# Linear attention, MoE and FFN on one core: the FFN's second weights converted during the MoE, and each expert's first product issued one branch earlier

## The chip, the cores and the metric

One core of a Trainium2 chip runs the whole program in one launch. The metric is the device time of one execution in microseconds (us). TensorE (PE) multiplies matrices, VectorE (DVE), ScalarE (ACT) and GpSimd (POOL) do elementwise work, SyncE (SP) issues DMA transfers, and ACT and POOL issue some too. Each engine works through its own instructions in order and waits on semaphores for the others.

## The reference

Three stages follow each other. Attention is linear: softmax of q over the head's elements, softmax of k over the sequence, `kv = k^T v`, and `q kv` per head. Its output, 4608 tokens of 512 elements, is the input of a mixture of experts: tokens with `x @ w_skip > 0` go to the expert with the highest gate logit,

```python
for e in range(8):
    h = np.maximum(xc[mask] @ w1[e], 0.0)          # 512 -> 1024
    y[mask] = gate_w[mask, None] * (h @ w2[e])     # 1024 -> 512
out[do_compute] = xc + y
```

and then comes a feed-forward network (FFN) over all tokens:

```python
h = x @ w_in                                        # 512 -> 2048
g = np.maximum(h, 0.0) + np.log1p(np.exp(-np.abs(h)))
return (g @ w_out).astype(np.float32)               # 2048 -> 512
```

The weights `w_in` and `w_out` come as 64-bit floats, passed as 64-bit integers. They have to be made float32 on the chip before they can be multiplied.

## The kernel before, in words

Every product is made of three: each operand is split into a high part h (rounded) and a low part l (the rest), and h·h, h·l and l·h are summed in PSUM. So each tile of tokens or weights costs an ACT copy (the high part) and a subtraction on DVE or POOL (the low part): `hilo` L494 to L498 for tokens, `split` L465 to L471 for an expert's weights, in eight pieces of 1024 columns.

Attention ends with a routing step that counts the tokens of each expert and scatters the rows into `xs` in DRAM, sorted by expert. The counts are known only at run time, so each expert is a tree of branches (`tiles`): tiles of 128 tokens are taken in pairs, and a branch asks whether there is another pair, another single tile, or none. On the given data the experts e0 to e7 have 4, 1, 2, 3, 1, 6, 5 and 8 tiles, which makes 2, 1, 1, 2, 1, 3, 3 and 4 pairs (a lone tile is counted as a pair here). For a pair, `mm1` (four steps of 24 matmuls, L522; for a lone tile `mm1one`, two halves of 12, L535) makes the hidden values in four PSUM banks `mph`; ACT's Relu and a DVE operation make their parts `mhT`, where a lone tile goes through the buffer `mh` first (Relu L536). Then `mm2` (L548 to L550) makes `mpy`, DVE adds it to the token rows (L553), and POOL scatters them back to `xs` (L555). While expert e computes, the weights of e+1 are split, a few pieces at a time, at places (`tick`) inside `mm1` and `mm2`; the order of all instructions is the order of the code. The weights of e+2 are loaded into the same staging buffers as they come free.

A 64-bit weight is converted by `Convert` (L416 to L433): two ACT operations (Abs and a copy of the low words, L423 and L424), four on DVE (L428 to L431) and two on POOL (L432, L433). The `w_in` words are converted in e7 by `cv`, 16 steps of 512 columns. The `w_out` words are converted in the FFN, again 16 steps of 512, one in each of the first 16 of its steps.

The FFN takes nine blocks of 512 tokens, each with 16 steps of 128 hidden columns, 144 steps in all. A step is `mm1` (12 matmuls L690), the softplus (three ACT operations L692 to L694, four DVE operations L697 to L701), the parts `gh` (ACT, L708) and `gl` (L712), and `mm2` of two steps earlier (12 matmuls each of L720 to L722). In the first 16 steps `mid` and `end` put in the conversion: `hi` L745 and `lo` L747 make the parts of a converted piece of `w_out`, `begin` and `end` (L748 to L751) convert another, and `rawload` L743 fetches 512 KB of words.

Of the kernel before, what the change touches and what calls it, by code (L numbers as in the profile page):

```python
# [76 lines left out]
def attention(tc, ctx, q, k, v, wg, xs, ident, consts):  # L77
    nc=tc.nc
# [309 lines left out]
    def finish(p):  # L388
# [22 lines left out]
        return nv,fence(list(writes)),others  # L411
# [5 lines left out]
class Convert:  # L417
# [7 lines left out]
    def rest(s):  # L425
        t,H,L=s.t,s.H,s.L; ti=t.bitcast(I32); Hf=H.bitcast(F32); Lf=L.bitcast(F32)
        v=s.nc.vector; p=s.nc.gpsimd
        v.tensor_scalar(t,t,LEAST,None,op0=ALU.max)  # L428
        v.tensor_scalar(ti,ti,3,0x3ffffff8,op0=ALU.logical_shift_left,op1=ALU.bitwise_and)  # L429
        v.scalar_tensor_tensor(out=ti,in0=H,scalar=-0x40000000,in1=ti,op0=ALU.bitwise_and,op1=ALU.bitwise_or)  # L430
        v.tensor_scalar(H,ti,-0x800000,None,op0=ALU.bitwise_and)  # L431
        p.tensor_tensor(out=Hf,in0=Lf,in1=Hf,op=ALU.mult)  # L432
        p.tensor_tensor(out=t,in0=t,in1=Hf,op=ALU.add)  # L433


KLV=5
LAG=3
ALL=[getattr(mybir.EngineType,x) for x in ("PE","Activation","DVE","Pool","SP")]
class Moe:
    def __init__(s, tc, ctx, xs, wsets, w64, ident, slotpool, spare, KLV=KLV):  # L440
        s.tc=tc; s.nc=tc.nc; s.xs=xs; s.users={}; s.w=wsets; s.ident=ident; s.w64=w64; s.K=KLV
# [38 lines left out]
    def cv(s,k=1):  # L480

        for _ in range(k):
# [44 lines left out]
    def mm1one(s,e,tick=lambda:None,between=lambda:None):  # L527

        nc=s.nc; wh,wl=s.slot[e]; xh,xl=s.xT[:,0,0],s.xT[:,1,0]
        for half in range(2):  # L530
            p=s.ph()
            ops=[(kc,x,w) for kc in range(4) for x,w in ((xh,wh),(xh,wl),(xl,wh))]
            if half==0: ops.sort(key=lambda o:o[1] is xl)
            for n,(kc,x,w) in enumerate(ops):
                nc.tensor.matmul(p,x[:,kc*128:kc*128+128],w[:,kc*1024+half*512:kc*1024+half*512+512],start=(n==0),stop=(n==11))  # L535
            nc.scalar.activation(s.h[:,half*512:half*512+512],p,AF.Relu)  # L536
            tick()
        for q in range(2):
            p=s.ph()
# [18 lines left out]
    def tiles(s,e,i,t):  # L558
# [3 lines left out]
        def second(last=None):  # L562
            for j in range(t): s.mm2(e,x[j],j,tick)
            if i==0: s.pieces(16)
            if last: last()
        def next():
            if i==0: s.late(e)
            s.first(e+1)
        if t==1:
            s.mm1one(e,tick,next); s.hint(e+1)  # L570
# [4 lines left out]
        def more(k):  # L575
            y=s.pair(e,i+1)
            for j in range(k): s.loadx(e,i+1,j)
            if i==0: s.late(e)
# [276 lines left out]
```

## Time and profile before

| | us |
|---|---|
| median of 3 runs | 1438.57 |
| lowest, highest | 1432.34, 1439.16 |
| profiled execution | 1438.16 |
| its span | 1434.9 |
| TensorE busy in the span | 1351.4 (94%) |
| VectorE busy | 867.4 (60%) |
| ScalarE busy | 640.9 (45%) |
| GpSimd busy | 299.4 (21%) |

The span is the time from the first to the last recorded instruction; 3.3 us of the execution lie around it. The first 160 us or so are attention, the experts reach to 569.4, and the FFN starts its first product at 580.84. A busy share over the whole span mixes these stages, so the rows below are taken from stretches of it.

### The profile page before, as it was taken

How to read it: one execution, taken by the hardware profiler on the slowest of the kernel's cores; microseconds unless marked ns; L12 is line 12 of the kernel's file. 1: busy time of each engine (PE TensorE's matmuls, PEld its weight loads, DVE VectorE, ACT ScalarE, POOL GpSimd, SP SyncE). 2: the span in 40 equal slices, each digit the busy share in tenths (PEclk: the TensorE clock that was granted, in tenths of full speed). 3: DMA queues.
4: the chain of work that ended last, by engine and by line, in shares of the span. 5: the costliest groups of instructions: out<-in, count | busy, mean ns of one | idle time of the engine just before them, and what ended most of it. 6: DMA issues, size and time to landing. Idle time of an engine off the chain costs nothing.

```text
span 1434.9 us, 19479 instructions
## 1 busy us (share of the span) xinstructions
PE 1351.4 (94%) x6951; PEld 1124.7 (78%) x6951; DVE 867.4 (60%) x1492; ACT 640.9 (45%) x1148; POOL 299.4 (21%) x371
## 2 busy tenths in 40 slices
PE   7999688999999989788999999999999999999998
PEld 7888686877988878566788888888888888888886
DVE  7996653436242794799655555555555555555554
ACT  5775432434131452555444444444444444444443
POOL 6587701112011553566200000000000000000000
PEclk9999799999999999999999999999999999999999
DMA  9764683547141422331100101001001010010000
GB/s 390 295 243 153 220 266 122 195 158 246 66 156 50 132 67 75 91 102 58 59 0 1 59 1 45 15 1 59 0 9 52 0 59 1 0 59 1 30 1 29
DMA packets 37939, 127.95 MB, mean 89 GB/s; under 512 B 5082, under 2 KB 5594, under 8 KB 34816
## 3 DMA queue, kind: packets, MB, share of 16 engines
q1 hardware_dynamic: 22192, 72.69, 14.8%
q10 hardware_dynamic: 9648, 34.10, 7.2%
q0 software_dynamic: 5920, 19.08, 3.6%
q8 instruction: 75, 1.23, 0.3%
q14 instruction: 104, 0.85, 0.2%
HBM read 97.34 MB, written 29.44 MB: 88 GB/s over the span
## 4 chain that ended last, share of the span: by engine, by line
PE 63%; DVE 10%; issue 2%; POOL 1%; ACT 1%; DMA 1%; another core or an unknown queue 1%; ACTq 0%; SPq 0%; DVEq 0%; POOLq 0%
PE h L690 25%; PE y L722 9%; PE y L721 9%; PE y L720 8%; PE mph L522 5%; PE mpy L548 2%; PE mpy L550 2%; PE mpy L549 2%; DVE d L698 1%; PE pt L679 1%; DVE l L701 1%; DVE cvt L428 1%; DVE mcvt L428 1%; DVE w0l L488 1%; DVE cvt L429 1%
## 5 line engine op out<-in xcount | busy, mean ns | idle before, releaser
L692 ACT ACTIVATE a<-h 128x512 f32<-128x512 f32 x144 | 86.2, 599 | 412.5 <-PE h L690 391.6
L697 DVE TENSOR_SCALAR d<-a 128x512 f32<-128x512 f32 x144 | 63.5, 441 | 314.9 <-ACT a L693 314.9
L722 PE MATMUL y<-w1h,gl 128*128 128x512 f32 x576 | 230.5, 400 | 17.0 <-POOL gl L712 13.1
L690 PE MATMUL h<-xh,w0h 128*128 128x512 f32 x576 | 231.1, 401 | 0.7 <-ACT xh L680 0.7
L721 PE MATMUL y<-w1l,gh 128*128 128x512 f32 x576 | 228.7, 397 | 0.0
L720 PE MATMUL y<-w1h,gh 128*128 128x512 f32 x576 | 228.1, 396 | 0.4 <-ACT gh L708 0.4
L690 PE MATMUL h<-xh,w0l 128*128 128x512 f32 x576 | 228.0, 396 | 0.0
L690 PE MATMUL h<-xl,w0h 128*128 128x512 f32 x576 | 227.8, 396 | 0.2 <-DVE xl L681 0.2
L722 PEld LDWEIGHTS y<-w1h,gl 128*128 128x128 f32 x576 | 109.0, 189 | 48.1 <-POOL gl L712 17.9
L721 PEld LDWEIGHTS y<-w1l,gh 128*128 128x128 f32 x576 | 108.6, 189 | 26.7
L720 PEld LDWEIGHTS y<-w1h,gh 128*128 128x128 f32 x576 | 108.6, 189 | 26.6 <-ACT gh L708 1.0
L690 PEld LDWEIGHTS h<-xh,w0l 128*128 128x128 f32 x576 | 108.6, 188 | 26.4
L690 PEld LDWEIGHTS h<-xl,w0h 128*128 128x128 f32 x576 | 108.7, 189 | 25.3 <-DVE xl L681 0.5
L690 PEld LDWEIGHTS h<-xh,w0h 128*128 128x128 f32 x576 | 108.5, 188 | 25.4 <-ACT xh L680 0.9
L698 DVE SCALAR_TENSOR_TENSOR d<-d,a 128x512 f32<-128x512 f32 x144 | 110.8, 769 | 5.0
L701 DVE TENSOR_TENSOR l<-d,l 128x512 f32<-128x512 f32 x144 | 101.9, 708 | 1.6
L699 DVE SCALAR_TENSOR_TENSOR d<-h,d 128x512 f32<-128x512 f32 x144 | 99.5, 691 | 4.9
L522 PE MATMUL mph<-mxT,w1h 128*128 128x256 f32 x512 | 94.3, 286 | 7.0 <-DVE w1l L469 4.7
L694 ACT ACTIVATE l<-a 128x512 f32<-128x512 f32 x144 | 91.3, 634 | 9.8 <-POOL gl L712 4.6
L524 ACT ACTIVATE mhT<-mph 128x512 fp32r<-128x512 f32 x52 | 30.8, 596 | 141.7 <-PE mph L522 88.1
L693 ACT ACTIVATE a<-a 128x512 f32<-128x512 f32 x144 | 91.0, 632 | 4.6
L712 DVE TENSOR_TENSOR gl<-l,gh 128x512 fp32r<-128x512 f32 x130 | 88.9, 683 | 0.7 <-ACT gh L708 0.7
(191 smaller groups left out, 2399.7 us busy)
## 6 DMA issues: line engine op xcount, KB each, us to landing
mst<-in_wsets_dram ACTq DMA_DIRECT2D x30, 512.0 KB, 4.4
vb<-in_v_dram SPq DMA_DIRECT2D x8, 1290.0 KB
spare<-in_wsets_dram ACTq DMA_DIRECT2D x18, 512.0 KB, 5.9
x<-xs SPq DMA_DIRECT2D x36, 256.0 KB, 3.9
q<-in_q_dram SPq DMA_DIRECT2D x8, 1024.0 KB, 9.5
spare<-in_w_dram SPq DMA_DIRECT2D x16, 512.0 KB, 3.8
mx<-xs SPq DMA_DIRECT2D x29, 264.0 KB, 2.9
k<-in_k_dram SPq DMA_DIRECT2D x7, 1024.0 KB, 18.8
```

Source lines behind the costliest of these rows:

```text
L522: nc.tensor.matmul(o,w[:,kc*1024+f*128:kc*1024+f*128+128],x[:,:,kc*128:kc*128+128],start=(n==0),stop=(n==11))
L690: nc.tensor.matmul(p,w[:,st],x[:,kc],start=(n==0),stop=(n==11)); n+=1
L692: nc.scalar.activation(a,p,AF.Abs)
L693: nc.scalar.activation(a,a,AF.Exp,scale=-1.0)
L694: nc.scalar.activation(l,a,AF.Ln,bias=1.0,scale=1.0)
L698: nc.vector.scalar_tensor_tensor(out=d,in0=d,scalar=-1.0,in1=a,op0=ALU.mult,op1=ALU.add)
L699: nc.vector.scalar_tensor_tensor(out=d,in0=p,scalar=0.0,in1=d,op0=ALU.max,op1=ALU.add)
L701: nc.vector.tensor_tensor(out=l,in0=d,in1=l,op=ALU.add)
L712: (nc.gpsimd if pool else nc.vector).tensor_tensor(out=gl,in0=l,in1=gh.bitcast(F32),op=ALU.subtract)
L720: nc.tensor.matmul(p,gh[:,st],wout[0][:,mv],start=(f==0),stop=False)
L721: nc.tensor.matmul(p,gh[:,st],wout[1][:,mv],start=False,stop=False)
L722: nc.tensor.matmul(p,gl[:,st],wout[0][:,mv],start=False,stop=(f==15))
```

## The change

There are three parts.

1. **The conversion of `w_out` leaves the FFN.** Each pair of tiles of the experts e0 to e6 takes one step (`task`): 690 columns of `w_out` (NB=12 steps, each 682 columns further) are converted from `mcv` into `mh`, the buffer that a lone tile uses for its hidden values. `keep` on SP stores the result to `wo` in DRAM (353 KB) and fetches the next 706 KB of words. In a pair that is the expert's first one, or a lone tile, all eight operations stand together behind the last pieces of weights in the middle of the last tile's `mm2`; in other pairs of two, DVE's part is in the first tile's `mm2` and POOL's two operations follow at its end. `plan` and `planned` work out from the counts which step each expert begins with; `remainder` converts what is left after e7 (here nothing, since e0 to e6 have 13 pairs). The FFN loads finished pieces of 256 KB from `wo`; its low part `lo` and `gl` are all on DVE now, where half of `lo` and most of the first block's `gl` were on POOL.
2. **The first product of the next expert** (`head`: the first quarter of `mm1`, or the first half of `mm1one`) is issued at the end of the preceding expert's branch, in an If of its own. `mm1` and `mm1one` leave it out for an expert's first pair. There are now two hints (head and two) for each expert.
3. **The pieces of the next expert's weights** stand a little earlier: two in the middle of the first tile's `mm2`, two at its end, all that are left in the middle of the last tile's.

```diff
+NB=12; WB=690; SB=682
+        s.mcv=bp.tile([128,1536],F32,name="mcv"); s.cn=18; s.ct={}; s.bg=None
+    def words(s): return s.mcv[:,0:2*WB].bitcast(I32)
+    def task(s,k):
+        if s.bg is None: s.bg=Convert(s.nc,s.words().rearrange("p (n w) -> p n w",w=2),s.h[:,0:WB]).steps()
+        for f in s.bg[:k]: f()
+        s.bg=s.bg[k:]
+    def fetch(s,n):
+        s.nc.sync.dma_start(s.words(),s.w64[1][:,bass.ds(s.step(n)*SB,WB)].bitcast(I32))
+    def keep(s,n):
+        assert s.bg==[]; s.bg=None
+        s.nc.sync.dma_start(s.wo[:,bass.ds(s.step(n)*SB,WB)],s.h[:,0:WB])
+        s.fetch((n[0],n[1]+1))
+    def planned(s):
+        s.first_task=[0]+[s.nc.values_load(s.firsts[0:1,e:e+1],[mybir.EngineType.SP],min_val=0,max_val=8*s.K) for e in range(6)]
+    def remainder(s):
+        s.left=s.nc.values_load(s.firsts[0:1,8:9],min_val=0,max_val=NB)
+        with s.tc.If(s.left<NB):
...
+    def head(s,e):
+        if e>=E: return
+        with s.tc.If(s.nv[e]>128,label=f"head{e}") as c: s.product(e,0,True)
+        with c.Else(): s.half(e,0)
+    def mm1(s,e,head,tick):
         for b in range(0,8,2):
...
+            if b or not head: s.product(e,b)
...
         def second(last=None):
-            for j in range(t): s.mm2(e,x[j],j,tick)
+            c=[0]
+            def both():
+                c[0]+=1
+                if e==7: return tick()
+                if i==0: s.pieces(16 if c[0]==2*t-1 else 2)
+                if i==0 or t==1:
+                    if c[0]==2*t-1: s.task(6)
+                elif c[0]<3: s.task(6-2*c[0])
+            for j in range(t): s.mm2(e,x[j],j,both)
             if i==0: s.pieces(16)
+            if e<7: s.keep((e,i))
             if last: last()
...
         def end():
-            next(); s.hint(e+1); second(lambda: s.cv(18))
+            next(); s.hint(e+1); second(lambda: s.cv(18)); s.head(e+1)
...
+            s.head(0)
+            s.fetch((0,0))
+            for e in range(E):
+                s.expert(e)
+                if e==0: s.planned()
+            s.remainder()
...
-        back_lo(j==0 and f>1)
+        back_lo()
...
+    def wload(f):
+        if f>=16: return
+        cv[f]=cp.tile([128,512],F32,tag="cvt",name="cvt")
+        nc.sync.dma_start(cv[f],wo[:,f*512:f*512+512])
...
     def lo(f):
         sl=slice(f*512,f*512+512)
-        (nc.vector if f%2 else nc.gpsimd).tensor_tensor(out=wout[1][:,sl],in0=cv[f].t,in1=wout[0][:,sl].bitcast(F32),op=ALU.subtract)
+        nc.vector.tensor_tensor(out=wout[1][:,sl],in0=cv[f],in1=wout[0][:,sl].bitcast(F32),op=ALU.subtract)
-    for f in range(3): rawload(f)
     loadx(0)
-    for f in range(2): begin(f); end(f)
+    for f in range(3): wload(f)
...
         def mid():
-            if n<16: hi(n); begin(n+2)
+            if n<16: hi(n)
         mm1(j,f,mid)
-        if n<16: lo(n); end(n+2)
+        if n<16: lo(n); wload(n+3)
```

Three places show how the change moves instructions. The first is TensorE at the start of e2, in the branch for two tiles. `mph_2215` is the first of the four PSUM banks and `mph_2216` the second, `mxT` the tokens, `w0h` and `w0l` the parts of the expert's weights. Before, from the branch on the number of tiles (L644):

```order
L644 COMPARE_AND_BRANCH
L572 REGISTER_ALU
L851 BRANCH_PREFETCH_HINT
L522 MATMUL mph_2215<-mxT,w0h 128x256 [waits DVE_49,Activation_49]
L522 MATMUL mph_2215<-mxT,w0l 128x256 [waits DVE_49]
L522 MATMUL mph_2215<-mxT,w0h 128x256
L522 MATMUL mph_2215<-mxT,w0l 128x256 [waits DVE_49]
L522 MATMUL mph_2215<-mxT,w0h 128x256
L522 MATMUL mph_2215<-mxT,w0l 128x256 [waits DVE_49]
L522 MATMUL mph_2215<-mxT,w0h 128x256
L522 MATMUL mph_2215<-mxT,w0l 128x256 [waits Pool_49]
L522 MATMUL mph_2215<-mxT,w0h 128x256 [waits DVE_49]
```

And now:

```order
L717 COMPARE_AND_BRANCH
L639 REGISTER_ALU
L922 BRANCH_PREFETCH_HINT
L565 MATMUL mph_2216<-mxT,w0h 128x256 [waits Activation_49]
L565 MATMUL mph_2216<-mxT,w0h 128x256 [waits DVE_49]
L565 MATMUL mph_2216<-mxT,w0l 128x256
L565 MATMUL mph_2216<-mxT,w0h 128x256 x2
L565 MATMUL mph_2216<-mxT,w0l 128x256
L565 MATMUL mph_2216<-mxT,w0h 128x256 x2
L565 MATMUL mph_2216<-mxT,w0l 128x256
L565 MATMUL mph_2216<-mxT,w0h 128x256 x2
L565 MATMUL mph_2216<-mxT,w0l 128x256 [waits Pool_49]
```

The first product is gone from here (it stands in the branch before), and the expert now begins with its second, which waits for DVE at its second matmul and for POOL at its twelfth.

The second place is ACT at the second pair of e3, a lone tile (`mh` its hidden values, `mph` the PSUM banks, `spare` the staging of weights). Before:

```order
L468 CAST w0h<-spare_2192 128x1024
L458 DMA mst_2224<-in_wsets_dram 128x1024 [waits DMAHW3_49,DVE_49]
L458 DMA spare_2190<-in_wsets_dram 128x1024 [waits DMAHW4_49,DVE_49]
L458 DMA spare_2191<-in_wsets_dram 128x1024 [waits DMAHW5_49,DVE_49]
L458 DMA spare_2192<-in_wsets_dram 128x1024 [waits DMAHW6_49,DVE_49]
L536 ACTIVATE mh<-mph_2215 128x512 [waits PE_49]
L536 ACTIVATE mh<-mph_2216 128x512 [waits PE_49]
L496 CAST mhT<-mph_2217 128x4x128 [waits PE_49]
```

And now:

```order
L474 CAST w0h<-spare_2193 128x1024
L464 DMA mst_2225<-in_wsets_dram 128x1024 [waits DMAHW0_49,DVE_49]
L464 DMA spare_2191<-in_wsets_dram 128x1024 [waits DMAHW1_49,DVE_49]
L464 DMA spare_2192<-in_wsets_dram 128x1024 [waits DMAHW2_49,DVE_49]
L464 DMA spare_2193<-in_wsets_dram 128x1024 [waits DMAHW3_49,DVE_49]
L423 ACTIVATE mh<-mcv 128x690
L424 ACTIVATE mcv<-mcv 128x690 [waits DMASW3_49]
L591 ACTIVATE mh<-mph_2215 128x512 [waits DMAHW4_49,PE_49,Pool_49]
L591 ACTIVATE mh<-mph_2216 128x512 [waits PE_49]
L541 CAST mhT<-mph_2217 128x4x128 [waits PE_49]
```

Between the last load and the Relu stand the two ACT operations of the first pair's conversion, and the Relu waits for POOL and for a transfer as well, the store of `mh` to `wo`.

The third place is DVE in the first block of the FFN, from one low part of `w_out` (`w1l`) to the step behind it (`d`, `a`, `h`, `l` belong to the softplus). Before:

```order
L747 TENSOR_TENSOR w1l<-cvt,w1h 128x512 [waits Activation_49]
L428 TENSOR_SCALAR cvt<-cvt 128x512 [waits Activation_49]
L429 TENSOR_SCALAR cvt<-cvt 128x512 [waits DVE_49]
L430 SCALAR_TENSOR_TENSOR cvt<-spare_2191,cvt 128x512 [waits DMAHW4_49,DVE_49]
L431 TENSOR_SCALAR spare_2191<-cvt 128x512 [waits DVE_49]
L697 TENSOR_SCALAR d<-a 128x512 [waits Activation_49]
L698 SCALAR_TENSOR_TENSOR d<-d,a 128x512 [waits DVE_49]
L699 SCALAR_TENSOR_TENSOR d<-h,d 128x512 [waits DVE_49]
L701 TENSOR_TENSOR l<-d,l 128x512 [waits DVE_49,Activation_49]
```

And now:

```order
L822 TENSOR_TENSOR w1l<-cvt,w1h 128x512 [waits DMAHW7_49,Activation_49]
L772 TENSOR_SCALAR d<-a 128x512 [waits DVE_49,Activation_49]
L773 SCALAR_TENSOR_TENSOR d<-d,a 128x512 [waits DVE_49]
L774 SCALAR_TENSOR_TENSOR d<-h,d 128x512 [waits DVE_49]
L787 TENSOR_TENSOR gl<-l,gh 128x512 [waits Activation_49]
L776 TENSOR_TENSOR l<-d,l 128x512 [waits DVE_49]
```

The four operations of the conversion are gone, `gl` has come over from POOL, and a low part of `w_out` stands in each step instead of in every other one.

## Rows read from the trace of the kernel before

**Rows 1.** The page: engines over the whole span, and DVE in 40 slices
```profile
PE 1351.4 (94%) x6951; PEld 1124.7 (78%) x6951; DVE 867.4 (60%) x1492; ACT 640.9 (45%) x1148; POOL 299.4 (21%) x371
DVE  7996653436242794799655555555555555555554
```

**Rows 2.** Windows of the FFN: length, then PE, PEld, DVE, ACT, POOL busy
```profile
580.84:694.54 113.70, 93.00 (x377) 70.25 (x378) 103.02 (x133) 63.81 (x111) 71.22 (x51) 0.97 0.23 69
694.54:785.60 91.06, 91.06 (x400) 73.45 (x400) 51.97 (x86) 41.53 (x71) 1.11 (x1) 1.00 0.07 24
```

**Rows 3.** The chain in time: start, length, piece (FFN)
```profile
605.49 1.42 DVE d L698
612.66 1.42 DVE d L698
...
694.54 2.79 PE h L690 x12
700.14 2.81 PE h L690 x12
```

**Rows 4.** DVE groups in the FFN's first block (busy, mean ns)
```profile
L698 DVE SCALAR_TENSOR_TENSOR d<-d,a 128x512 f32<-128x512 f32 x16 | 22.2, 1388 | 0.5
```

**Rows 5.** The same in its second block
```profile
L698 DVE SCALAR_TENSOR_TENSOR d<-d,a 128x512 f32<-128x512 f32 x16 | 11.1, 692 | 0.6
L747 DVE TENSOR_TENSOR w1l<-cvt,w1h 128x512 fp32r<-128x512 f32 x1 | 0.7, 678 | 0.0
```

**Rows 6.** TensorE's timeline in e0: second pair's tokens
```profile
189.31 0.66 PE L510 MATMUL mpt<-ident,mx 128*128 128x128 f32 x4 [1.74 <-DMA mx<-xs]
```

**Rows 7.** The page: DMA issues, KB each, us to landing
```profile
mst<-in_wsets_dram ACTq DMA_DIRECT2D x30, 512.0 KB, 4.4
x<-xs SPq DMA_DIRECT2D x36, 256.0 KB, 3.9
mx<-xs SPq DMA_DIRECT2D x29, 264.0 KB, 2.9
```

**Rows 8.** TensorE's timeline where experts begin
```profile
230.83 0.47 PE L535 MATMUL mph<-w1h,mxT 128*128 128x512 f32 x1 [2.87 <-issue]
...
247.27 0.28 PE L522 MATMUL mph<-mxT,w0h 128*128 128x256 f32 x1
...
250.54 0.97 PE L522 MATMUL mph<-mxT,w0h 128*128 128x256 f32 x6 [2.17 <-DVE w0l L469]
...
275.77 0.36 PE L522 MATMUL mph<-mxT,w1h 128*128 128x256 f32 x1 [2.52 <-DVE w1l L469]
...
315.36 0.47 PE L535 MATMUL mph<-w0h,mxT 128*128 128x512 f32 x1 [0.17 <-issue]
```

**Rows 9.** DVE's timeline from e1 to e2
```profile
244.85 1.22 DVE L469 TENSOR_TENSOR w0l<-spare,w0h 128x1024 fp32r<-128x1024 f32 x1
247.47 0.75 DVE L553 SCALAR_TENSOR_TENSOR mx<-mpy,mx 128x512 f32<-128x512 f32 x1 [1.40 <-PE mpy L550]
248.14 2.35 DVE L469 TENSOR_TENSOR w0l<-spare,w0h 128x1024 fp32r<-128x1024 f32 x2
```

**Rows 10.** One conversion of 512 columns in e7: ACT's group
```profile
L423 ACT ACTIVATE mcvt<-mst 128x512 f32<-128x512 f32 x10 | 6.7, 674 | 0.0
```

**Rows 11.** DVE's timeline of it, first and last of its four
```profile
471.69 0.42 DVE L428 TENSOR_SCALAR mcvt<-mcvt 128x512 f32<-128x512 f32 x1
...
473.33 0.43 DVE L431 TENSOR_SCALAR mst<-mcvt 128x512 int32<-128x512 int32 x1
```

**Rows 12.** POOL's timeline of it
```profile
473.90 1.04 POOL L432 TENSOR_TENSOR mst<-mst 128x512 f32<-128x512 f32 x1 [7.13 <-ACT mhT L524]
475.01 1.31 POOL L433 TENSOR_TENSOR mcvt<-mcvt,mst 128x512 f32<-128x512 f32 x1
```

**Rows 13.** DVE's timeline in e3, second half of the first pair
```profile
298.02 2.35 DVE L469 TENSOR_TENSOR w0l<-spare,w0h 128x1024 fp32r<-128x1024 f32 x2
```

**Rows 14.** ACT's timeline in e3: the lone tile's first Relu
```profile
305.13 0.60 ACT L536 ACTIVATE mh<-mph 128x512 f32<-128x512 f32 x1 [6.10 <-PE mph L535]
```

More of the change, by code (lines that the diff above doesn't have):

```diff
@@ L410, in finish @@
         for e in range(1,E): count(e)
-        return nv,fence(list(writes)),others
+        return nv,fence(list(writes)),others,counts
     return finish,ends
@@ new lines, in step, with plan @@
+    def step(s,n): return (s.first_task[n[0]]+n[1])%NB if n[0] else n[1]%NB
+    def fetch(s,n):
[4 more added lines that the diff above has]
+        s.fetch((n[0],n[1]+1))
+    def plan(s):
+        v=s.nc.vector; one=lambda a,n: s.mcv[0:1,2*WB+a:2*WB+a+n]; K=s.K
+        lim,gt,num,sums,ones=one(0,8*K),one(8*K,8*K),one(16*K,8),one(16*K+8,8),one(16*K+16,8)
+        te=lambda t: t.rearrange("p (t e) -> p t e",t=K)
+        for t in range(K): v.memset(one(8*t,8),256.0*t)
+        v.memset(ones,1.0)
+        v.tensor_tensor(out=te(gt),in0=bm(s.counts,K),in1=te(lim),op=ALU.is_gt)
+        v.tensor_reduce(num,gt.rearrange("p (t e) -> p e t",t=K),axis=AX.X,op=ALU.add)
+        v.tensor_tensor_scan(sums,ones,num,0.0,ALU.mult,ALU.add)
+        v.tensor_copy(s.firsts[:,0:8],sums)
+        v.tensor_scalar(s.firsts[:,8:9],sums[:,6:7],float(NB),None,op0=ALU.min)
@@ L526, in mm1, with mm1one @@
             tick(b)
-    def mm1one(s,e,tick=lambda:None,between=lambda:None):
-        nc=s.nc; wh,wl=s.slot[e]; xh,xl=s.xT[:,0,0],s.xT[:,1,0]
+    def mm1one(s,e,head,tick=lambda:None,between=lambda:None):
+        nc=s.nc
         for half in range(2):
[L531 to L536, printed above, removed]
+            if half or not head: s.half(e,half)
+            nc.scalar.activation(s.h[:,half*512:half*512+512],s.ph[half],AF.Relu)
             tick()
         for q in range(2):
-            p=s.ph()
+            p=s.ph[2+q]
             for c in range(4): nc.tensor.transpose(p[:,c*128:c*128+128],s.h[:,q*512+c*128:q*512+c*128+128],s.ident)
@@ L567, in next @@
             if i==0: s.late(e)
+            if (e,i)==(0,0): s.plan()
             s.first(e+1)
         if t==1:
-            s.mm1one(e,tick,next); s.hint(e+1)
-            return second(lambda: s.cv(18))
+            s.mm1one(e,i==0,tick,next); s.hint(e+1)
+            second(lambda: s.cv(18))
+            return s.head(e+1)
         if i+1<s.K: tc.mark_branch_hint_location(f"more{e}_{i}",hint=n>256*(i+1)+128,engines=ALL)
@@ L582, in end @@
         def end():
-            next(); s.hint(e+1); second(lambda: s.cv(18))
+            next(); s.hint(e+1); second(lambda: s.cv(18)); s.head(e+1)
         if i+1==s.K:
             with tc.If(n>256*(i+1)) as c:
-                second(lambda: s.cv(18)); s.rest(e,256*(i+1)); s.first(e+1)
+                second(lambda: s.cv(18)); s.rest(e,256*(i+1)); s.first(e+1); s.head(e+1)
             s.restore(todo)
@@ L622, in warm @@
     def warm(s):
[L624 to L625 removed]
+        for n,b in enumerate(s.done[:5]):
+            p=s.ph[n%4]
             for c in range(4): after(s.tc,s.nc.tensor.transpose(p[:,c*128:c*128+128],s.ident,s.ident),b)
@@ L629, in run @@
         with tc.manual_schedule():
-            s.nv,f0,others=finish(s.pT()); s.rows=[f0]
+            s.nv,f0,others,s.counts=finish(s.pT()); s.rows=[f0]
             s.warm()
@@ L635, in run @@
             s.rows+=[others(s.first(0))]*(E-1)
-            for e in range(E): s.expert(e)
+            s.head(0)
[4 more added lines that the diff above has]
+            s.remainder()
             for c in range(56): s.nc.tensor.transpose(s.pT.t[c%2][:,0:128],s.ident,s.ident)
@@ L649, in expert, with ffn @@
             with d.Else():
-                s.late(e); s.pieces(16); s.cv(18); s.first(e+1)
+                s.late(e); s.pieces(16); s.cv(18); s.first(e+1); s.head(e+1)
+                if e==0: s.plan()
     def hint(s,e):
-        if e<E: s.tc.mark_branch_hint_location(f"two{e}",hint=s.nv[e]>128,engines=ALL)
+        if e<E:
+            for x in ("head","two"): s.tc.mark_branch_hint_location(f"{x}{e}",hint=s.nv[e]>128,engines=ALL)
 FLAG=2
-def ffn(tc, ctx, xs, rows, out, wraw, win, wout, ident, spare):
+def ffn(tc, ctx, xs, rows, out, wo, win, wout, ident, spare):
     nc=tc.nc
```

84 lines of the change are left out of this document (45 added, 39 removed).

## The prediction

> **What bounds the kernel now.** I read the page first. TensorE is busy for 94% of the span and DVE for 60% [rows 1], so over the whole span it is a TensorE kernel; but DVE's slices show where it is not. Before the long row of fives come slices with 7, 9, 9: they lie at the end of the experts and the beginning of the FFN, and there DVE is at its limit. The next view is therefore busy time by windows. The FFN's first block takes 113.70 us, in which DVE is busy 103.02 and TensorE 93.00; the second block, with the same work on tokens and no conversion, takes 91.06 with TensorE busy all of it and DVE 51.97 [rows 2]. The chain of waits says the same: in the first block it runs through DVE's softplus operation, which comes every 7.17 us (605.49 to 612.66), in the second through the products, with a step every 5.60 us (694.54 to 700.14), half of it the 12 matmuls of h [rows 3]. So the first block is bound by DVE, the rest of the FFN by TensorE. Among the experts, TensorE waits in short pieces where one expert ends and the next begins: 2.87, 2.17, 2.52 us, sometimes almost nothing [rows 8]. Two of them are ended by DVE's low part of the new expert's weights.
>
> **The FFN's first block.** What goes: the conversion (two ACT, four DVE, two POOL operations in each of the first steps) with its raw loads. What stays on DVE: the softplus, `gl`, and now a low part in each step. The second block shows this load almost exactly: 51.97 us of DVE in 16 steps, 3.25 a step, with `gl` on DVE already [rows 2]; a low part adds 0.68 [rows 5]. 3.9 us is below the step's 5.60, so TensorE sets the pace. POOL is empty, and DVE's operations return to their undisturbed length, as 1388 ns beside a busy POOL is 692 without [rows 4, 5]. The window holds 16 products h but only 14 products y, since y runs two steps behind. At 2.80 each (half of 5.60) that is 84.0; the four tokens' transposes are what the second block has over 32 products, 91.06 - 89.6 = 1.5. So 85.5. At the start the first y waits for `gl`: behind the second h stand two ACT operations of about 0.6 [rows 14] and four on DVE of up to 0.69 [rows 5], together 3.8, beside a third h of 2.8: 1.0 of waiting. 113.7 - 86.5 = 27.2; I take 26, because the loads of finished pieces follow right behind the first tokens and may delay them. The bounds are 27 and 21 (the first tokens or pieces late by a landing of 3.9 us [rows 7] and some more). A piece of 256 KB takes such 3.9 us, is loaded three steps ahead, and so stays hidden.
>
> **What the experts pay.** A conversion of 690 columns costs, by those of 512 in e7 times 690/512: Abs 0.91 [rows 10], DVE's four (471.69 to 473.76, 2.07) 2.8 [rows 11], POOL's two (473.90 to 476.32, 2.42) 3.3 [rows 12]. The busy time of all 13, 36 us on DVE and 43 on POOL, lies beside TensorE's work; what counts is who waits for the end of this chain of 7.0 us.
>
> Beginnings of e2, e3 and e5: the pair before is an expert's only one, so its conversion stands as late as it can, and the second product waits for POOL. From e1 to e2: before, DVE's last two pieces come behind the last add, at 248.14, though DVE is free from 246.1 [rows 9]. Now they precede it and end at 248.5; Abs to 249.4, DVE to 252.2, POOL to 255.5. The wait is at the twelfth matmul of the second product, which before would have run at 247.27 + 2.8 + 2.17 + 1.4 = 253.6 [rows 3, 8]. So TensorE no longer loses 2.17 in the first product and loses 1.9 more than it did in the second. For e3, with two tiles and earlier pieces, I expect about 1: +1.5 for each of the three, +4.5 in all. Bounds: -1.5 each where the old stall goes and nothing comes, +3 where DVE and POOL slow each other.
>
> e3's second pair, a lone tile, writes its hidden values to `mh`, where the first pair's converted words lie until they are stored. Before, the Relu came at 305.13 as soon as its product was done [rows 14]. Now DVE has four pieces and one add ahead of the conversion; two pieces end at 300.4 [rows 13], the last can follow to 301.6; then 0.2 for the loads behind it, Abs to 302.7, DVE to 305.5, POOL to 308.7, and the store of 353 KB, for which I take 3.5, between 264 KB in 2.9 and 512 KB in 4.4 [rows 7]: 312.2. That is +7.0; bounds 3 (pieces done earlier) and 9.
>
> e4 is a lone tile too, and its Relu waits for the store of e3's last pair and the fetch behind it. By the same chain, with everything 7.0 later, POOL ends there at about 324, the store lands at 327.5, the 706 KB at 329.8 (5.6 by the slope of [rows 7]), and the first half, issued early, is done at about 325 (315.36 [rows 8] + 7.0 + 2.8). 2.5 by the store, 4.8 by the fetch; the mean of 3.6, with bounds 0 and 7.
>
> e0: the first fetch of 706 KB stands on SP ahead of the second pair's tokens, which TensorE waits for already, 1.74 us [rows 6]. At 1.5 us for 248 KB [rows 7] the words take 4.3 alone, shared with the tokens some 2: +2.0, bounds 0 and 4.3.
>
> The head: at e1 TensorE stood 2.87 us in issue [rows 8]. Half a product now runs ahead of this gap; the instruction that follows still has to be reached, so I take only -1.0 (-2.9 to +1). For the other heads, the price is one more branch. The rows have 0.17 for a branch into an expert and 2.87 for another [rows 8]; near the low one, 0.4 at five places where no other wait covers it, +2.0 (0 to 23). For the register loads on SP, the branch behind e7 and e7's first conversion, which waits for the last fetch, +1.0 (0 to 4): the wait behind it reaches TensorE only where DVE bounds e7.
>
> **Sum.** -26.0 + 4.5 + 7.0 + 3.6 + 2.0 - 1.0 + 2.0 + 1.0 = -6.9, against the profiled execution's 1438.16: 1431.3. The median of the three runs is 1438.57, 0.4 above it, which changes nothing. I predict 1431 us.
>
> **Rivals.** *The waits are covered* (0.24): the conversions end before anyone needs them, and the three beginnings, e3 and e4 cost nothing. For it speaks that DVE and POOL are far from full among the experts; against it that the order puts the waits in front of TensorE with a chain of 7 us behind 3 us of work. -6.9 - 15.1 = -22: 1416.
>
> *Conversions and pieces get in each other's way* (0.16). In the FFN DVE's operation beside a busy POOL takes twice as long [rows 4, 5]. If at each of the five places where the chain is waited for one more pair of POOL operations, 2.4 us [rows 12], has to be waited out, that is +12: 1443, no change. The Trainium skill (SBUF — State Buffer, Who interferes with whom) says that DVE and GpSimd share a pair of ports as an exclusive lock, and whichever comes second stands for the whole instruction of the first; by that a collision would cost a whole POOL operation each time, which is this rival, and the doubled operation in the FFN agrees with it while the free stretches of POOL between pairs speak for few collisions.
>
> *The added branches* (0.10), which ends slower. Each of the eight heads is a branch with a join more than before. If each cost what stood in front of e1, 2.87, the heads would cost 23 in place of my 2.0: 1431 + 21 = 1452. It decides from 2.1 us a head on (16.8 / 8), above which the kernel is slower by over 0.5%. For it speaks that one gap; against it 0.17 in front of e4, with the same kind of branch [rows 8]. The Trainium skill (Runtime: NRT & Kernel Launch, Instruction fetch mechanics) says that a taken branch out of the fetched window has to wait for a DMA fetch of its target; by that rule each head not hinted right stands for a fetch, which is this rival. The 2.87 agrees, the 0.17 does not.
>
> **From cases to numbers.** My forecast has 0.50, with a range of its own of 1424 to 1438. A change below 0.5%, 7 us, can't be told from none with this kernel: faster is below 1431.4, slower above 1445.8. The forecast lies at the first bound, so 0.28 of its 0.50 are faster and 0.22 the same; the covered waits are all faster (0.24); of the collisions 0.13 are the same and 0.03 slower; the branches slower (0.10). Faster 0.52, same 0.35, slower 0.13. From 1414 to 1445 the range holds the forecast, the covered waits and most collisions, and leaves the branches out.
>
> **What would show it.** Right: in the FFN's first block DVE's busy share near 0.7, steps of 5.6 us, about 87 us for the block; TensorE stalls of 2 to 4 us in the second product of e2, e3 and e5, ended by POOL's memset or DVE; a stall of 6 to 8 us in e3's lone tile ended by ACT behind a DMA on `mh`. Wrong: issue gaps above 2 us behind each head; a first block above 92 us; or no stall at all in e3.

## The result, and the profile after

The changed kernel takes 1452.64 us (median of 4, 1450.59 to 1455.49); the kernel before, timed beside it, 1435.45. The ratio is 1.0127, with a 95% interval of 1.0091 to 1.0164: slower by 1.3%, where I had forecast 0.5% faster and a range that ends at 1445.

The page after, with busy time, DVE and the granted clock in 40 slices (tenths of full speed):

```profile
PE 1359.6 (94%) x6951; PEld 1134.7 (78%) x6951; DVE 850.3 (59%) x1513; ACT 643.4 (44%) x1142; POOL 260.0 (18%) x343
...
DVE  7997654545434379466655555555555555555554
...
PEclk9999799998998999999999999999999999999999
```

Against [rows 1] the two nines that DVE had in the FFN's first block (the 18th and 19th slices) are sixes; the nine that is left in the middle belongs to e7. What the page hides is that TensorE is busy for 8.2 us more, with the same number of instructions. Windows split the span into the experts (e0's first product to the end of e7's last second product), the FFN's first block and its second: length, then busy time of PE, PEld, DVE, ACT, POOL, then the granted clock.

```profile
174.27:609.22 434.95, 383.57 (x2209) 335.48 (x2210) 230.30 (x311) 155.14 (x226) 136.17 (x138) 0.94 0.49 159
621.33:709.11 87.78, 86.63 (x377) 69.34 (x378) 57.95 (x97) 47.83 (x83) 0.00 (x0) 1.00 0.18 52
709.11:800.17 91.06, 91.06 (x401) 73.44 (x400) 52.11 (x87) 41.50 (x71) 0.00 (x0) 1.00 0.07 24
```

The experts of the kernel before, which [rows 2] do not have:

```profile
174.03:569.24 395.21, 367.90 (x2208) 322.90 (x2209) 198.39 (x249) 136.87 (x204) 98.12 (x112) 0.97 0.44 143
```

The first block went from 113.70 [rows 2] to 87.78: 25.9 us gained. The experts went from 395.21 to 434.95: 39.7 lost. With half a microsecond more between the two stages, 0.4 more behind the first block and 0.2 ahead of e0, that is the 15.0 by which the span grew (1434.9 to 1449.9). The loss has two parts that the windows separate: TensorE is idle for 51.4 us (434.95 - 383.57) in place of 27.3, +24.1, and the same matmuls keep it busy for 383.57 in place of 367.90, +15.7, at a clock of 0.94 in place of 0.97.

What the idle time waits for, from the summary of TensorE's waits in the experts (total, times, longest), after:

```profile
PE mpt L555 <- DMA mx<-xs: 11.8, 7, 3.2
PE mph L565 <- issue: 9.0, 3, 4.4
...
PE mph L595 <- ACT mh L591: 5.8, 2, 3.8
PE mph L572 <- issue: 4.0, 1, 4.0
PE mpt L555 <- issue: 3.8, 2, 2.1
PE mph L565 <- DVE mx L608: 3.6, 2, 2.3
PE mph L565 <- POOL mapart L609: 2.3, 2, 1.2
PE mpt L555 <- DVE w1l L475: 1.6, 1, 1.6
```

And before:

```profile
PE mph L522 <- DVE w1l L469: 4.7, 2, 2.5
PE mph L535 <- issue: 3.0, 2, 2.9
PE mpt L510 <- issue: 3.0, 2, 1.6
PE mph L522 <- issue: 2.8, 3, 1.8
...
PE mph L522 <- DVE w0l L469: 2.2, 1, 2.2
PE mpt L510 <- DMA mx<-xs: 1.7, 1, 1.7
```

The stalls on pieces of weights, 6.9, have become 5.9 on DVE and POOL in the second product. New are 10.1 on tokens, 5.8 on the lone tiles' hidden values, and 8.0 more of issue. These places on TensorE's timeline show how they look: the tokens of e0's second pair, the beginnings of e2 (two waits) and e3, the lone tile of e3, e4, the tokens of e5, the two gaps at the beginning of e6, and the tokens of its lone tile (in brackets the idle time before, and what ended it):

```profile
190.42 0.66 PE L555 MATMUL mpt<-ident,mx 128*128 128x128 f32 x4 [2.23 <-DMA mx<-xs]
192.68 0.69 PE L555 MATMUL mpt<-ident,mx 128*128 128x128 f32 x4 [1.60 <-DMA mx<-xs]
...
259.41 0.39 PE L565 MATMUL mph<-mxT,w0h 128*128 128x256 f32 x1 [2.27 <-DVE mx L608]
...
262.01 0.58 PE L565 MATMUL mph<-mxT,w0l 128*128 128x256 f32 x1 [1.15 <-POOL mapart L609]
...
290.78 0.79 PE L565 MATMUL mph<-mxT,w1h 128*128 128x256 f32 x2 [4.42 <-issue]
...
325.05 0.66 PE L595 MATMUL mph<-ident,mh 128*128 128x128 f32 x4 [3.83 <-ACT mh L591]
...
341.87 0.66 PE L595 MATMUL mph<-ident,mh 128*128 128x128 f32 x4 [2.00 <-ACT mh L591]
...
372.15 1.32 PE L555 MATMUL mpt<-ident,mx 128*128 128x128 f32 x8 [2.49 <-DMA mx<-xs]
...
439.38 0.79 PE L565 MATMUL mph<-mxT,w0h 128*128 128x256 f32 x2 [2.78 <-issue]
...
443.23 0.37 PE L565 MATMUL mph<-mxT,w0l 128*128 128x256 f32 x1 [1.78 <-issue]
...
480.19 1.09 PE L555 MATMUL mpt<-ident,mx 128*128 128x128 f32 x4 [3.22 <-DMA mx<-xs]
```

The clock's part shows in windows of single stretches: e0's `mm2` behind the late tokens, and the rest of e6's first product behind its two gaps.

```profile
193.09:206.09 13.00, 13.00 (x53) 10.38 (x52) 6.48 (x7) 5.86 (x7) 1.82 (x4) 0.87 0.96 349
...
443.23:453.58 10.35, 10.35 (x66) 10.35 (x66) 3.79 (x4) 3.07 (x4) 0.00 (x0) 0.71 0.18 55
```

Before, the same 48 matmuls of e0 took 11.45 at clock 1.00, and the same ones of e6, with no gap ahead of them, 7.70:

```profile
189.72:201.17 11.45, 11.45 (x53) 9.23 (x52) 5.95 (x7) 4.78 (x5) 0.76 (x3) 1.00 0.95 314
...
409.03:416.73 7.70, 7.70 (x68) 7.70 (x67) 5.64 (x6) 3.91 (x5) 0.00 (x0) 1.00 0.48 146
```

So 2.1 us more of waiting for tokens (2.23 + 1.60 against 1.74 [rows 6]) were followed by 1.55 us of slower matmuls, and the two gaps of e6 by 2.65; a granted clock of 0.87 means that a part of this stretch ran at 1.2 GHz and the rest at 2.4.

### The profile page after: what moved, and what is told of

Its sections match the earlier page's. It is cut to its first block, busy times and chain, and to the rows that moved or that the text cites. A ratio compares the mean times of both kernels' runs of the same rounds, so it can differ in the third digit from the quotient of the medians.

```text
span 1449.9 us, 19690 instructions
## 1 busy us (share of the span) xinstructions
PE 1359.6 (94%) x6951; PEld 1134.7 (78%) x6951; DVE 850.3 (59%) x1513; ACT 643.4 (44%) x1142; POOL 260.0 (18%) x343
## 3 DMA queue, kind: packets, MB, share of 16 engines
q8 instruction: 78, 1.28, 0.4%
## 4 chain that ended last, share of the span: by engine, by line
PE 62%; DVE 5%; DMA 4%; issue 2%; another core or an unknown queue 1%; ACT 1%; POOL 1%; SPq 0%; ACTq 0%; POOLq 0%; DVEq 0%
PE h L765 27%; PE y L797 9%; PE y L796 9%; PE y L795 9%; DMA xs<-mx 3%; PE mph L565 3%; PE pt L754 1%; PE mpy L603 1%; PE mpy L605 1%; PE mpy L604 1%; DVE mcv L430 1%; DVE w0l L494 1%; DVE mcv L431 1%; DVE mcv L432 1%
## 5 line engine op out<-in xcount | busy, mean ns | idle before, releaser
L773 DVE SCALAR_TENSOR_TENSOR d<-d,a 128x512 f32<-128x512 f32 x144 | 99.7, 693 | 5.0
L776 DVE TENSOR_TENSOR l<-d,l 128x512 f32<-128x512 f32 x144 | 98.6, 685 | 0.1
L787 DVE TENSOR_TENSOR gl<-l,gh 128x512 fp32r<-128x512 f32 x144 | 98.1, 682 | 0.7 <-ACT gh L783 0.7
L565 PEld LDWEIGHTS mph<-mxT,w1h 128*128 128x128 f32 x512 | 81.4, 194 | 8.3 <-issue 4.6
## 6 DMA issues: line engine op xcount, KB each, us to landing
vb<-in_v_dram SPq DMA_DIRECT2D x8, 1290.0 KB, 15.7
```

The costliest lines, as they stand in the source:

```text
L565: s.nc.tensor.matmul(o,w[:,kc*1024+f*128:kc*1024+f*128+128],x[:,:,kc*128:kc*128+128],start=(n==0),stop=(n==11))
L773: nc.vector.scalar_tensor_tensor(out=d,in0=d,scalar=-1.0,in1=a,op0=ALU.mult,op1=ALU.add)
L776: nc.vector.tensor_tensor(out=l,in0=d,in1=l,op=ALU.add)
L787: nc.vector.tensor_tensor(out=gl,in0=l,in1=gh.bitcast(F32),op=ALU.subtract)
```

## The experiments

Four theories stood against each other: A, each head's branch costs an issue gap; B, SP stands in the store until POOL is done, and the branches and tokens' loads behind it come late; C, the transfers' traffic; D, the conversion's own work. Beside the time I read from each profile the stretch from e0's first product to the end of e7's last second product, and TensorE's busy time in it:

| kernel | experts, us | busy | idle | median | before beside it | ratio, 95% interval |
|---|---|---|---|---|---|---|
| before | 395.2 | 367.9 | 27.3 | | | |
| changed | 435.0 | 383.6 | 51.4 | 1452.64 | 1435.45 | 1.0127 (1.0091 to 1.0164) |
| x1_head | 396.2 | 367.9 | 28.3 | 1435.74 | 1430.85 | 1.0034 (1.0014 to 1.0054) |
| x2_nohead | 435.9 | 382.8 | 53.1 | 1448.27 | 1430.85 | 1.0123 (1.0107 to 1.0140) |
| x3_keeppool | 432.6 | 382.0 | 50.6 | 1446.01 | 1430.85 | 1.0116 (1.0084 to 1.0148) |
| x4_ffn | 387.1 | 364.1 | 23.0 | 1401.33 | 1430.85 | 0.9796 (0.9775 to 0.9816) |
| y1_nodma | 413.6 | 376.8 | 36.8 | 1424.39 | 1430.58 | 0.9942 (0.9923 to 0.9961) |
| y2_dmaonly | 401.3 | 370.2 | 31.1 | 1417.57 | 1430.58 | 0.9905 (0.9873 to 0.9936) |
| y3_mh | 429.6 | 378.6 | 51.0 | 1443.17 | 1430.58 | 1.0088 (1.0058 to 1.0119) |
| y4_dve6 | 419.1 | 373.9 | 45.3 | 1436.95 | 1430.58 | 1.0038 (1.0015 to 1.0061) |
| z1_all | 417.4 | 378.5 | 38.9 | 1436.49 | 1435.14 | 1.0012 (0.9993 to 1.0031) |
| z2_allnh | 415.9 | 375.5 | 40.4 | 1435.25 | 1435.14 | 1.0000 (0.9975 to 1.0025) |
| z3_pooldve | 424.6 | 378.4 | 46.2 | 1441.87 | 1435.14 | 1.0051 (1.0033 to 1.0069) |
| y5_early | 434.8 | 382.8 | 52.0 | 1446.85 | 1430.38 | 1.0106 (1.0077 to 1.0135) |
| z4_early | 429.9 | 381.2 | 48.7 | 1440.82 | 1430.38 | 1.0074 (1.0052 to 1.0096) |
| z5_earlynh | 425.6 | 380.7 | 44.8 | 1441.09 | 1430.38 | 1.0068 (1.0043 to 1.0092) |

x4_ffn has the experts of the kernel before: 387.1 against 395.2 is what two profiles of one code differ by, so differences of the stretch below 8 us say little by themselves, and the timed ratios have to bear them out.

**The parts of the change, one at a time.** Heads alone (with the conversion taken out of the experts and the FFN of before):

```diff
-            if e<7: s.keep((e,i))
-                if i==0 or t==1:
-                    if c[0]==2*t-1: s.task(6)
-                elif c[0]<3: s.task(6-2*c[0])
```

> Heads alone: the next expert's first product one branch earlier and the pieces in their new places, but no conversion among the experts and the FFN as before. Theory A (the extra branch costs TensorE an issue gap, as at e1, e3 and e6 of the changed kernel, 4.05, 4.42 and 2.78 + 1.78 us): 8 to 11 us slower than before, with these gaps in its trace. Theory B (the gaps come from engines that arrive late at the branch, above all SP, which stands at the store of converted words): the gaps are not here, within 3 us of before, or up to 5 us faster because the stalls of 2.17 and 2.52 us on pieces of weights get cover.

And the changed kernel without them:

```diff
     def head(s,e):
-        with s.tc.If(s.nv[e]>128,label=f"head{e}") as c: s.product(e,0,True)
-        with c.Else(): s.half(e,0)
+        return
-            if b or not head: s.product(e,b)
+            s.product(e,b,first=(b==0 and head))
```

> The changed kernel with each first product back in its own branch and one hint per expert. Theory A (branches): about 11 us faster than the changed kernel (1441 to 1443), no gap above 1 us at e3 and e6. Theory B (late engines, SP at the store): within 4 us of the changed kernel, gaps of the same size at the one branch that is left.

Theory A's forecasts fail from both sides. Heads alone are 4.9 us slower than the kernel before (1435.74 against 1430.85, 2 to 8 by the interval), not 8 to 11, and the stretch of the experts shows 1.0 of it (396.2, 395.2 without). Taking the heads out of the changed kernel leaves 435.9 (435.0) and a ratio of 1.0123 (1.0127). But theory B's forecast for x1_head fails too, for the gaps are there, 3.33 us at e3 and 3.46 at e1 (put down to ACT, whose part was done 0.8 us before the matmul; the branch ahead of it took 3.61), in place of the stalls on weights. They are TensorE's own branch instructions, and the kernel before has them as well. These are two of its branches, DVE's last piece of weights for e3, and the branch of the head of e3 in the changed kernel (for a branch its count, the shortest, median and longest in ns, and the first and last start):

```profile
L644 PEldq COMPARE_BRANCH  x8: 65/71/2973, 173.4 to 464.8; - x8
L593 PEldq COMPARE_BRANCH  x1: 6071/6071/6071, 268.9 to 268.9; - x1
273.96 1.22 DVE L469 TENSOR_TENSOR w1l<-spare,w1h 128x1024 fp32r<-128x1024 f32 x1
...
L576 PEldq COMPARE_BRANCH  x1: 5994/5994/5994, 284.1 to 284.1; - x1
```

Matmuls issued ahead of such a branch run on beside it, and only what is left of it is a gap: 0.17 us in front of e4 [rows 8], where the branch at 312.08 took the 2.97; 2.52 of 6.07 in front of e3, put down to DVE, whose piece was done at 275.18, 0.6 before the matmul; 4.42 of 5.99 at e3 now, where 2.3 us of matmuls were left to run when the branch began, in place of 4.3. What heads cover they give back: without them the summary of waits has 13.0 us on POOL in the first products, where the changed kernel has 2.3.

```profile
PE mpt L555 <- DMA mx<-xs: 13.7, 8, 4.3
PE mph L565 <- POOL mapart L607: 13.0, 4, 4.2
PE mph L593 <- ACT mh L589: 7.8, 2, 5.3
```

The FFN alone, with its pieces from other weights:

```diff
-            ffn(tc, ctx, xs, m.rows[-1], out, wo, m.slot[8], m.slot[9], ident, spare)
+            ffn(tc, ctx, xs, m.rows[-1], out, wsets[7], m.slot[8], m.slot[9], ident, spare)
```

> The experts as before and the FFN of the changed kernel, with its pieces loaded from the weights of the last expert: the conversion of the second weights is left out. If the FFN's term stands by itself: 25 to 27 us faster than before (ratio 0.982), first block 86 to 88 us. Rival (the loads of pieces right behind the first tokens make the FFN begin later): 20 to 23 us faster.

Faster by 29.5 us between the medians (26 to 32 by the interval), a little more than expected, though its first block takes 89.5 in place of 113.70, 24.2 less; where the rest of the 29.5 lies I did not find. This part of the change does what it should; some 25 to 30 is also all that there is to win.

**Work and transfers of the conversion.** Without the stores and the later fetches, and with them but without the eight operations:

```diff
-        s.nc.sync.dma_start(s.wo[:,bass.ds(s.step(n)*SB,WB)],s.h[:,0:WB])
-        s.fetch((n[0],n[1]+1))
```

> The changed kernel without the stores to wo and the fetches after the first: the conversions run on words that are there already, and the FFN takes its pieces from the weights of the last expert (the second weights are left out). Theory B (the waits behind the store are the larger part): SP is free, so the tokens' loads are early again and the lone tiles wait for POOL alone. Of the 40 us that the experts lost, 22 to 28 come back: 1420 to 1430. Theory D (the conversions' own time on DVE, ACT and POOL is what costs): at most 12 come back, 1440 or more.

```diff
-                if i==0 or t==1:
-                    if c[0]==2*t-1: s.task(6)
-                elif c[0]<3: s.task(6-2*c[0])
```

> The changed kernel with all stores and fetches and no conversion at all (whatever lies in mh is stored): the transfers' traffic and the place of their issues by themselves. Theory B: the store has no POOL operation to wait for, so SP is in time; the cost of the experts falls from 40 to under 12 us, 1415 to 1424. Theory C (traffic, or the lone tile's wait on the store's landing): 15 us or more of the 40 stay.

Measured against x1_head's 396.2, which has heads and no conversion, the transfers alone cost 5.1 us, the work alone 17.4, both together 38.8: 16.3 appear only where both are there. The timed ratios, taken from x4_ffn's 0.9796, or from that and x1_head's 0.0034, give 11 to 16 for the transfers, 16 to 21 for the work, 42 to 47 for both, which leaves 11 to 16. Both runs are faster than the kernel before, as the work alone, or the transfers alone, cost less than the FFN gains, and both times are as theory B had them. C as the whole cause falls, and D explains less than half. The chain, in which the transfers have to follow the work, is the simplest reading of what is left, and not the larger part either; that transfers and work slow each other directly would show in the same term.

**Shortening the chain at its links.** Its two last operations on DVE:

```diff
-        if s.bg is None: s.bg=Convert(s.nc,s.words().rearrange("p (n w) -> p n w",w=2),s.h[:,0:WB]).steps()
+        if s.bg is None: s.bg=Convert(s.nc,s.words().rearrange("p (n w) -> p n w",w=2),s.h[:,0:WB]).steps(s.nc.vector)
```

> The changed kernel with the conversion's last two operations on DVE (0.9 us each, by the others of two inputs) in place of POOL (1.34 + 1.67). The chain behind which the second product, the store, SP and the last tile's scatter stand is 1.2 us shorter each time and POOL's own scatter free. Theory B: 6 to 12 us faster than the changed kernel, from e2, e3, e5 and the tokens at e6. Theory D (time on DVE itself): slower, by 2 to 8 us, the DVE waits at e2 and e5 (2.27, 1.28) longer.

```profile
170.62:589.75 419.13, 373.85 (x2208) 327.77 (x2209) 251.97 (x337) 154.59 (x226) 98.83 (x112) 0.96 0.50 165
```

This is the largest single effect: 15.8 us less in the experts, 6.1 of them waiting and 9.7 busy time, though DVE has 21.7 us more to do (251.97 against 230.30). The ratio falls from 1.0127 to 1.0038, some 12.7 us, at the upper end of theory B's forecast; the profiled execution, 1431.43, was a fast one. A collision of the two engines does not show. DVE's third operation of a conversion and POOL's two in the changed kernel, then DVE's third and DVE's own last two here (busy time, mean ns):

```profile
L432 DVE SCALAR_TENSOR_TENSOR mh<-mcv,mh 128x690 int32<-128x690 int32 x13 | 11.4, 879 | 1.2
L434 POOL TENSOR_TENSOR mcv<-mcv 128x690 f32<-128x690 f32 x13 | 17.4, 1338 | 58.7 <-DVE mcv L433 27.1 <-DMA spare<-in_wsets_dram 18.1 <-issue 4.6
L435 POOL TENSOR_TENSOR mh<-mh,mcv 128x690 f32<-128x690 f32 x13 | 22.0, 1694 | 1.0
...
L432 DVE SCALAR_TENSOR_TENSOR mh<-mcv,mh 128x690 int32<-128x690 int32 x13 | 11.4, 878 | 0.4
L434 DVE TENSOR_TENSOR mcv<-mcv 128x690 f32<-128x690 f32 x13 | 11.4, 875 | 0.9
L435 DVE TENSOR_TENSOR mh<-mh,mcv 128x690 f32<-128x690 f32 x13 | 11.4, 879 | 0.4
```

DVE's operation has the same length in both, as have its pieces of weights (1.22 to 1.25 us), and the last two take 1.75 us on DVE against 3.03 on POOL. That leaves the chain, 1.28 us shorter each time, and POOL's scatters, which no longer stand behind it.

Store and fetch issued by POOL in place of SP (the store's line; the fetch's is changed alike):

```diff
-        s.nc.sync.dma_start(s.wo[:,bass.ds(s.step(n)*SB,WB)],s.h[:,0:WB])
+        s.nc.gpsimd.dma_start(s.wo[:,bass.ds(s.step(n)*SB,WB)],s.h[:,0:WB])
```

> The changed kernel with the store of converted words and the fetch of the next ones issued by POOL, behind its own two operations, in place of SP. Theory B (SP waits in the store for POOL and what stands behind it on SP, branches and the tokens' loads, comes late): the waits for tokens at e0, e5 and e6 (2.23 + 1.60, 2.49 + 1.72, 3.22 us) go for the most part, 10 to 15 us faster than the changed kernel (1438 to 1443). Rival C (the transfers' traffic, or the scatter behind POOL's operations, makes the tokens late): within 4 us of the changed kernel. The waits of the lone tiles on the buffer mh (3.83 and 2.00 us) stay in either.

The place that theory B is about is in the trace of the changed kernel. SP in e6 stores, fetches and then loads the lone tile's tokens at 477.26, just when TensorE is ready for them; the store waited for POOL's memset behind the conversion, and behind the fetch SP passes two branches (in the form of the branches above):

```profile
470.38 0.36 SPq L513 DMA_DIRECT2D wo<-mh  x1
471.06 0.35 SPq L509 DMA_DIRECT2D mcv<-in_w_dram  x1
L658 SPq COMPARE_BRANCH  x1: 151/151/151, 471.6 to 471.6; - x1
L661 SPq COMPARE_BRANCH  x1: 57/57/57, 476.9 to 476.9; - x1
477.26 0.34 SPq L550 DMA_DIRECT2D mx<-xs  x1
```

From the first branch to the second lie 5.1 us in which SP waits for nothing that the trace shows; a store in time would have left room for them. Before, the same load was issued at 430.57, 9 us ahead of its use (439.98). But x3_keeppool has 432.6 all the same, and by its ratio the kernel is some 1.6 us faster, as rival C had it. Its waits for tokens fell from 11.8 to 3.9, and e0 became 9.8 us shorter (49.1 against 58.9, by its last second product); yet TensorE waited 5.54 and 4.96 for the two Relus in place of 3.83 and 2.00, and e7 became 5.8 longer (108.6 against 102.8: 2.4 idle, 3.4 in slower matmuls). So B names a real wait and not the cost: with SP free, the next link ends last. Why e7 waits longer I did not separate.

The lone tile's hidden values away from the converted words:

```diff
-NB=12; WB=690; SB=682
+NB=13; WB=632; SB=630
-            nc.scalar.activation(s.h[:,half*512:half*512+512],s.ph[half],AF.Relu)
+            for a,n in ((0,512),) if half==0 else ((0,384),(384,128)): nc.scalar.activation(hid(half*512+a,n),s.ph[half][:,a:a+n],AF.Relu)
```

> The changed kernel with the lone tile's hidden values in other places than the converted words (the pair's unused second token buffer, the rest of mh, the end of mcv), and 13 steps of 632 columns in place of 12 of 690 to make room. By my sum the two waits on mh cost 10 us: 9 to 12 us faster than the changed kernel, e3 near 45 us and e4 near 16 us long (50.6 and 20.0 before that). If other waits stand right behind these (DVE's pieces, the next tokens), 0 to 4 us.

By the ratio, 1.0088, this is some 5.6 us faster than the changed kernel, between the two forecasts. e3 got 7.5 us shorter (43.1 against 50.6) and e4 2.9 longer (22.9 against 20.0), since there the next tokens, which SP issued only at 328.30, took the place of the Relu:

```profile
332.08 1.30 PE L555 MATMUL mpt<-ident,mx 128*128 128x128 f32 x5 [7.71 <-DMA mx<-xs]
```

**All links together, and the place.** The three changes above, and no fetch behind e6's last pair; the same without heads; and without the moved hidden values:

```diff
-            if e<7: s.keep((e,i))
+            if e<7: s.keep((e,i),e<6 or last is None)
```

> The changed kernel with the waits taken away that the runs named: the conversion's last two operations on DVE, store and fetch issued by POOL, the lone tile's hidden values away from the converted words (13 steps of 632 columns), no fetch behind e6's last pair. If these were the cost and add up: MoE 23 to 29 us shorter than in the changed kernel, 1422 to 1430, 0 to 8 us faster than before. If the work on DVE and the transfers cost the rest wherever their waits stand: 1432 to 1438.

> The same without heads. With POOL's wait gone the second product has less to wait for, so the head's cover is worth less: within 4 us of the kernel with heads. If the extra branch costs at e6 (4 to 5 us there), up to 5 us faster.

> Conversion on DVE, store and fetch issued by POOL, but the lone tile in mh with the converted words, 12 steps of 690. The difference to the first of these three is the wait on mh by itself: 5 to 10 us if nothing else stands behind it, 0 to 3 if the tokens' loads do, as in the run that moved only the hidden values. 1428 to 1436.

The gains don't add: z1_all's 417.4 is y4_dve6's 419.1 within what profiles differ by, with less waiting (38.9 against 45.3) and more busy time. Its kernel and the one without heads are as fast as the one before, and not faster, which is the second of the two forecasts. Between z3 and z1 lie 5.4 us of the median (7.2 in the experts): TensorE waits 12.4 us for the lone tiles' Relus in z3 and not in z1, so this is the wait on `mh` once less stands behind it.

Last, the place. In pairs of two tiles the whole conversion goes ahead of the pieces, in the first tile's second products; in the changed kernel, and in z1 and z2:

```diff
-                if i==0 or t==1:
-                    if c[0]==2*t-1: s.task(6)
-                elif c[0]<3: s.task(6-2*c[0])
+                if t==2 and c[0]==1: s.task(6)
+                if t==1 and c[0]==1: s.task(6)
```

> The changed kernel with one thing moved: in pairs of two tiles all eight operations of the conversion stand in the middle of the first tile's second products, ahead of the pieces of weights, not behind them in the last tile's. If it is the late place that makes POOL's end, the store, SP and the next tokens late: e0, e3, e5 and e6 get back 12 to 18 us together, total 1436 to 1441. If it is the work on POOL and DVE wherever it stands: within 5 us of the changed kernel (e1 and e4, lone tiles, are not touched).

> All changes of z1 (DVE's six operations, transfers issued by POOL, hidden values elsewhere) and the early place. The wait of the second product on DVE's last operation at e3 (4.8 us gap) and the waits at e6 should shrink: 5 to 10 us faster than z1, that is 1426 to 1431 against a kernel before of 1435. If the gaps at the beginning of an expert are the branch's own: within 3 us of z1.

> The same without heads: equal to the one with heads within 3 us if the branch costs what the cover gives; 3 to 6 us faster if e6's gaps belong to the head's branch, as there the kernels without heads were 5 to 8 us shorter.

y5_early has 434.8, the changed kernel 435.0, and z4 and z5 are slower than z1 and z2, by 0.6 to 0.7%, where I had forecast z4 5 to 10 us faster: the late place was not it. Where the conversion comes early, the tokens come late: TensorE waits 18.4 us for them in y5_early (11.8 in the changed kernel) and 14.6 in z4_early (2.8 in z1_all). With heads and without, z4 and z5 are equal, as are z1 and z2.

## Why the prediction was wrong

*The FFN's term* was right: -26.0 forecast, 113.70 to 87.78 measured. DVE is busy for 66% of the block, steps are 5.6 us, and the first `y` waits 0.92 us for `gl` (1.0 in my working).

*The five places with a price* came out near as waiting, 13.3 us where I had 17.1. Beginnings of e2, e3 and e5: 10.3 us of waits there (2.27 + 1.15, 4.42, 1.28 + 1.15) against 6.9 before (4.7 and 2.2 in the summary), +3.4 where I had +4.5. At e2 and e5 the mechanism is the one forecast; at e3 it is a branch of TensorE in both kernels, where I had read DVE before and forecast POOL after, so that this place fits by luck. The lone tiles: second products begin 4.4 us later at e3 (7.0 forecast; the stall is 3.83 where I had 6 to 8) and 3.4 later at e4 (3.6). e0: +2.1 of waiting (2.0).

*The tokens of the later pairs* were not in the sum. I had SP's queue in e0 alone; the store stands on SP in all 13 pairs, behind POOL, and e5 and e6 waited 2.49, 1.72 and 3.22 us for tokens.

*The step that failed* is the sum itself: it added waiting, each term at the full clock, and nothing for the matmuls that follow a wait. I had 19 us of losses among the experts; the waits came to 24.1, and 15.7 us of slower matmuls came on top. From x4_ffn over the kernel before to the changed one, idle time goes 23.0, 27.3, 51.4 and busy time 364.1, 367.9, 383.6: 0.9 and 0.65 us more of busy time for each microsecond more of waiting. The stretches behind single waits at clocks of 0.87 and 0.71 show the link, and over the 16 rows of the table busy time rises with idle time by 0.58 us for each, but single runs stray from it (y3_mh, 51.0 idle, 378.6 busy), so it is no law. 26 gained against 24 would have been no change; with the clock it is 14 lost in the profile.

*The rivals.* The time landed on the 1452 of the added branches by luck, for the mechanism is another: issue adds 8.0 of the 24.1 us of waiting, and beside the conversion heads cost nothing on balance (x2 against the changed kernel, z1 against z2, z4 against z5; alone, 4.9 us in x1). My readings of its two prices were wrong: the 0.17 in front of e4 is what matmuls left uncovered of a branch of 2.97, not the price of a cheap branch. The Trainium skill (Runtime: NRT & Kernel Launch, Instruction fetch mechanics) says that a taken branch whose target lies outside the fetched window stalls until it is fetched; the trace agrees as far as that TensorE's branches take from 0.07 to 6.07 us. Such stalls were there before, and the trace does not bear out a further one for each head. The collisions did not come: DVE's operation of two inputs on 690 columns takes 879 ns with POOL in the chain and 878 in y4_dve6 without, so neither shows a wait for the other. The Trainium skill (SBUF — State Buffer, Who interferes with whom) says that whichever of the two engines comes second at the shared ports stands for the whole instruction of the first; among these conversions no such wait shows. What y4_dve6 gave back goes with the shorter chain and what hung on it.

What stays open is the 11 to 16 us that work and transfers cost only together: the links I took out (POOL's operations, SP's queue, `mh`) are real waits in the trace, and alone only POOL's operations gave back much; for the others another wait took their place, in whole or in part.

## What to carry to other kernels

Work moved under a stage that TensorE bounds is not free because the engines it runs on are half idle: price the whole chain up to what waits for its end, for each queue that it stands in (here ACT, DVE, POOL, SP and two transfers, 13 times). Read a gap at a branch from the branch instruction itself, and not from the idle time or from the engine that it is put down to. Where TensorE would have to wait, count the matmuls behind the wait too, from rows at either clock. And when a chain has several waits, take out all of them in one trial before believing in the largest: the next one is often as long.

## What the runs showed that I had not expected

In this kernel a microsecond of waiting on TensorE among the experts went with some 0.65 us of slower matmuls (15.7 beside 24.1). Moving two operations of each conversion from POOL to DVE, the engine with more to do, shortened the experts by 15.8 us in the profile and the kernel by some 12.7. And one and the same branch took TensorE 0.07 us or 2.97, of which the matmuls already issued can cover nearly all.
